# Batch-by-batch order, part of K and V kept on chip, four-byte transposes and column-tiled matmuls in a two-pass attention decode

## The chip, the cores and the metric

The kernel runs on one core of one Trainium2 chip. The metric is the device time of one execution in microseconds (us). A run with "rounds" alternates the kernel under test with the kernel before on the same chip. Ratios are the mean time of one kernel's runs over that of the other's runs of the same rounds, so they are not quite the ratio of the medians quoted.

TensorE does the matrix multiplies; the traces show each as two records, the load of a *stationary* operand and the matmul of a *moving* operand with it (25052 of each in the kernel before). VectorE and ScalarE do elementwise work and in these kernels copy results out of PSUM, TensorE's output memory (640 copies of 691 ns and 384 of 1012 ns for the transposes of the kernel before). GpSimd does the reduction over partitions (256 of them there, 371 or 430 ns each). DMA brings data from HBM, the chip's main memory (557 MB there).

## The reference, cut to what matters

Two identical rounds of attention and a feed-forward network (FFN) on 8 sequences, one token each. The K and V caches are the same in both attention passes, and 268 MB a pass; all else is small.

```python
B, Hq, Hkv, Sk, Dh, D, F = 8, 32, 8, 8192, 128, 512, 1792      # bf16
def attn(x):
    q = (x @ wq).reshape(B, 1, Hq, Dh).transpose(0, 2, 1, 3)
    k = repeat(k_cache, 4, axis=1);  v = repeat(v_cache, 4, axis=1)
    p = softmax(q @ k.T * Dh ** -0.5)
    return (p @ v) ... @ wo
x = x + attn(layernorm(x));  x = x + silu(layernorm(x) @ w1) @ w2
x = x + attn(layernorm(x));  x = x + silu(layernorm(x) @ w1) @ w2
```

One (batch, group) *pair* is a K of 8192 x 128 and a V of the same size, 2.1 MB each, and serves 4 query heads. There are 64 pairs a pass.

## The kernel before: the parts that matter

All 64 pairs of one pass, then the FFN, then all 64 pairs again. K has its positions on partitions when it lands; the scores take it the other way round, so each of its 64 chunks of 128 x 128 goes through TensorE as a bf16 transpose, 8 of them to one tile in PSUM, and is copied out by VectorE or ScalarE. Then K is the *stationary* operand of the scores, and V that of the PV product, with 4 moving columns each.

```python
def emit_tgroup(j, grp):                       # 8 transposes, one copy
    for k in range(CPG):
        pe.transpose(tpv[:, k, :], KNs[kn][:, c, :], ident[:, :])
    # copy of 128x1024 bf16 out of PSUM: ScalarE for groups 1, 4, 7, else VectorE
def emit_scores_group(j, grp):
    pe.matmul(scp[:, c, :], KTs[kt][:, c, :], QT[:, b, g*REP:(g+1)*REP])
...
for t in range(NPAIR + L_PV + 1):
    jp = t - L_PV
    for grp in range(GROUPS):
        emit_tgroup(t + 1, grp)                # K of the next pair
        emit_scores_group(t, grp)              # scores of this pair
        emit_pv_group(jp, grp)                 # PV of two pairs ago
        # softmax steps of pair t-1 at grp 1 and 4 ...
```

What TensorE is given in one step comes from three different pairs. A copy has a whole pair's time to finish before its scores come up.

## Time and profile before

| | before |
|---|---|
| time, median | 1409.9 us (3 runs; 1409.3 after a fourth) |
| bytes read | 557 MB |
| DMA rate over the span; in mid-pass | 400; 417 to 421 GB/s |
| TensorE busy | 90% |
| mean granted TensorE clock | 0.617 |

From the page of the kernel before: busy time of TensorE, then, in 40 slices of the span, the granted clock and DMA's busy share in tenths, the rate moved, the chain of waits by engine, and the two costliest groups of its transposes (busy us, mean ns of one | idle before).

```profile
span 1403.6 us, 53785 instructions
...
PE 1266.5 (90%) x25052; PEld 1235.7 (88%) x25052; DVE 673.8 (48%) x1436; ACT 450.6 (32%) x527; POOL 103.1 (7%) x263
...
PEclk8655556555657667567767855555575555667677
DMA  9999999999999999999499999999999999999981
GB/s 390 395 399 409 420 419 424 425 425 411 421 420 419 418 420 406 425 419 416 161 419 377 427 426 416 416 413 413 409 421 419 420 420 418 423 423 425 422 367 64
...
PE 61%; DMA 36%; issue 2%; DVE 0%; ACT 0%; SPq 0%; ACTq 0%; DVEq 0%
...
L386 PE MATMUL TPp<-ident,arena 128*128 128x128 bf16 x8192 | 937.6, 286 | 29.7 <-DMA arena<-in_A_k_cache_dram 19.0
...
L393 DVE COPY arena<-TPp 128x1024 bf16<-128x1024 bf16 x640 | 440.5, 691 | 505.1 <-PE TPp L386 498.8
```

The table of stretches of the same kernel (stretch and its length; busy us of TensorE, weight loads, VectorE, ScalarE, GpSimd with counts; granted clock, DMA share, GB/s):

```profile
200.00:400.00 200.00, 191.57 (x3760) 190.88 (x3758) 101.35 (x215) 66.67 (x78) 15.57 (x39) 0.57 1.01 421
...
800.00:1000.00 200.00, 200.00 (x3749) 200.00 (x3747) 101.61 (x215) 66.61 (x77) 15.63 (x39) 0.50 1.00 417
```

TensorE and DMA are at their limit at once: DMA moves 417 to 421 GB/s at a share of 1.00, and TensorE is busy without a gap, at half its clock in the second stretch. The chain of waits there, start and length of each piece in us, repeats every 1.28 us:

```profile
300.04 0.87 PE TPp L386 x8
300.91 0.19 PE SCp L439 x8
301.10 0.23 PE OTp L495 x8
301.33 0.87 PE TPp L386 x8
```

Eight such steps make a pair: 10.24 us. Where the clock was granted in full (1.00 from 785 to 788 us, 0.50 from 300 to 310 us), the same group of 8 transposes took half as long (timeline of the kernel before; start, length):

```profile
786.36 0.61 PE L386 MATMUL TPp<-ident,arena 128*128 128x128 bf16 x8 [1.94 <-issue]
786.81 0.34 PE L439 MATMUL SCp<-QT,arena 128*128 128x4 bf16 x8
```

The next group starts 0.45 us after the transposes: 56 ns each.

### The profile page before, as it was taken

The page shows a single profiled execution, that of the slowest core. Times are in us where ns is not written, and L with a number is a line of the kernel's source. Part 1 is how long each engine was busy: PE and PEld are TensorE (multiplying, and loading weights), DVE is VectorE, ACT ScalarE, POOL GpSimd, SP SyncE. Part 2 cuts the span into 40 slices and gives each one's busy share as a digit, 9 for nine tenths or more (in the row PEclk, how much of TensorE's full clock was granted, in tenths as well). Part 3 has the DMA queues.
Part 4 walks back from the last instruction along what each step waited for, and adds up shares of the span by engine and source line. Part 5 has one row for each costly group of instructions (what it writes and reads, how often), then busy time and mean ns, then how long its engine had stood idle before and what let it go on. Part 6 is the DMA issues. An engine that isn't in the chain of part 4 may idle for free.

```text
span 1403.6 us, 53785 instructions
## 1 busy us (share of the span) xinstructions
PE 1266.5 (90%) x25052; PEld 1235.7 (88%) x25052; DVE 673.8 (48%) x1436; ACT 450.6 (32%) x527; POOL 103.1 (7%) x263
## 2 busy tenths in 40 slices
PE   3999999999987888998758899999999999888987
PEld 2999999999987888988538799999999999888984
DVE  1554544554544445555325455555555544445552
ACT  1433323333323323333124333333333333233331
POOL 0000000000000000000000000000000000000000
PEclk8655556555657667567767855555575555667677
DMA  9999999999999999999499999999999999999981
GB/s 390 395 399 409 420 419 424 425 425 411 421 420 419 418 420 406 425 419 416 161 419 377 427 426 416 416 413 413 409 421 419 420 420 418 423 423 425 422 367 64
DMA packets 48767, 560.78 MB, mean 400 GB/s; under 512 B 4240, under 2 KB 14240, under 8 KB 14752
## 3 DMA queue, kind: packets, MB, share of 16 engines
q1 hardware_dynamic: 37440, 541.10, 92.1%
q10 hardware_dynamic: 11104, 16.25, 3.2%
q8 instruction: 196, 3.21, 0.9%
q14 instruction: 27, 0.22, 0.0%
HBM read 557.33 MB, written 0.01 MB: 397 GB/s over the span
## 4 chain that ended last, share of the span: by engine, by line
PE 61%; DMA 36%; issue 2%; DVE 0%; ACT 0%; SPq 0%; ACTq 0%; DVEq 0%
PE TPp L386 38%; DMA arena<-in_A_v_cache_dram 31%; PE OTp L495 12%; PE SCp L439 9%; DMA arena<-in_A_k_cache_dram 5%; PE MISC L544 1%; PE MISC L580 1%; DMA wreg<-in_A_wq_dram 1%; PE MISC L562 0%; DVE X L341 0%; ACT L311 0%; SPq L255 0%; ACT arena L391 0%; DVE xn L317 0%; DVE st_11 L307 0%
## 5 line engine op out<-in xcount | busy, mean ns | idle before, releaser
L386 PE MATMUL TPp<-ident,arena 128*128 128x128 bf16 x8192 | 937.6, 286 | 29.7 <-DMA arena<-in_A_k_cache_dram 19.0
L386 PEld LDWEIGHTS TPp<-ident,arena 128*128 128x128 bf16 x8192 | 712.3, 129 | 30.6 <-DMA arena<-in_A_k_cache_dram 19.2
L393 DVE COPY arena<-TPp 128x1024 bf16<-128x1024 bf16 x640 | 440.5, 691 | 505.1 <-PE TPp L386 498.8
L391 ACT COPY arena<-TPp 128x1024 bf16<-128x1024 bf16 x384 | 388.6, 1012 | 860.5 <-PE TPp L386 860.5
L495 PE MATMUL OTp<-P,arena 128*128 128x4 bf16 x8192 | 366.4, 168 | 70.6 <-DMA arena<-in_A_v_cache_dram 61.7
L439 PEld LDWEIGHTS SCp<-QT,arena 128*128 128x128 bf16 x8192 | 398.4, 111 | 8.9 <-issue 7.4
L439 PE MATMUL SCp<-QT,arena 128*128 128x4 bf16 x8192 | 394.9, 170 | 6.1 <-issue 5.2
L495 PEld LDWEIGHTS OTp<-P,arena 128*128 128x128 bf16 x8192 | 295.8, 102 | 77.6 <-DMA arena<-in_A_v_cache_dram 66.0
L455 POOL PARTITION_ALL_REDUCE mxa<-mxp x128 | 47.4, 371 | 832.9 <-DVE mxp L450 832.9
L460 DVE TENSOR_TENSOR SCs<-SCs,mxa 128x256 f32<-128x256 f32 x128 | 54.5, 426 | 72.5 <-POOL mxa L455 72.5
L481 POOL PARTITION_ALL_REDUCE ssa<-ssm x128 | 55.0, 430 | 430.4 <-DVE ssm L476 430.4
L468 ACT ACTIVATE P<-SCs 128x256 bf16<-128x256 f32 x128 | 53.5, 418 | 31.3 <-DVE SCs L460 31.3
L484 DVE RECIPROCAL rcp<-ssa 128x4 f32<-128x4 f32 x128 | 22.8, 178 | 71.2 <-POOL ssa L481 71.2
L450 DVE TENSOR_REDUCE mxp<-SCs 128x4 f32<-128x256 f32 x128 | 53.8, 420 | 4.3
L447 DVE COPY SCs<-SCp 128x256 f32<-128x256 f32 x128 | 53.1, 415 | 3.2 <-PE SCp L439 3.2
L476 DVE TENSOR_REDUCE ssm<-P 128x4 f32<-128x256 bf16 x128 | 52.4, 409 | 1.6 <-ACT P L468 1.6
L507 DVE TENSOR_TENSOR attnT<-OTp,rcp 128x4 bf16<-128x4 f32 x128 | 21.3, 167 | 10.2 <-PE OTp L495 10.2
L544 PE MATMUL MISC<-wreg,attnT 128*8 128x512 bf16 x64 | 19.1, 472 | 0.5 <-DVE attnT L507 0.5
L326 PEld LDWEIGHTS MISC<-ident,xn 8*128 8x128 bf16 x16 | 0.7, 94 | 20.9 <-DVE xn L317 20.9
L326 PE MATMUL MISC<-ident,xn 8*128 8x8 bf16 x16 | 1.0, 165 | 19.5 <-DVE xn L317 19.5
L544 PEld LDWEIGHTS MISC<-wreg,attnT 128*8 128x8 bf16 x64 | 6.4, 102 | 12.4 <-issue 7.1
L341 DVE TENSOR_TENSOR X<-MISC,X 8x512 bf16<-8x512 f32 x4 | 2.7, 678 | 29.0 <-PE MISC L544 19.3
(26 smaller groups left out, 56.5 us busy)
## 6 DMA issues: line engine op xcount, KB each, us to landing
arena<-in_A_k_cache_dram SPq DMA_DIRECT2D x128, 2048.0 KB, 15.8
arena<-in_A_v_cache_dram SPq DMA_DIRECT2D x128, 2048.0 KB, 20.3
wreg<-in_A_wo_dram ACTq DMA_DIRECT2D x2, 4096.0 KB, 160.6
wreg<-in_A_wq_dram SPq DMA_DIRECT2D x2, 2048.0 KB, 7.5
wreg<-in_A_wq_dram ACTq DMA_DIRECT2D x2, 2048.0 KB, 19.6
w_5<-in_B_w_dram ACTq DMA_DIRECT2D x1, 1792.0 KB, 28.7
w_6<-in_B_w_dram ACTq DMA_DIRECT2D x1, 1792.0 KB, 96.1
X<-in_A_x_dram SPq DMA_DIRECT2D x1, 8.0 KB
```

Of the source, the lines that this page charges most:

```text
L386: lambda k=k, c=c: pe.transpose(tpv[:, k, :], KNs[kn][:, c, :], ident[:, :])
L391: op(act, lambda: act.copy(dst, tpv), reads=[r_TPp[tb]], writes=[r_KTg[kt][grp]])
L393: op(dve, lambda: dve.tensor_copy(dst, tpv), reads=[r_TPp[tb]], writes=[r_KTg[kt][grp]])
L439: lambda c=c: pe.matmul(scp[:, c, :], KTs[kt][:, c, :], rhs, start=True, stop=True)
L447: op(dve, lambda: dve.tensor_copy(SCs[sl][:, :, :], scp), reads=[r_SCp[bank]], writes=[r_SCs[sl]])
L450: lambda: dve.tensor_reduce(mxp[sl][:, :], SCs[sl][:, :, :], AX.X, ALU.max),
L455: lambda: pool.partition_all_reduce(mxa[sl][:, :], mxp[sl][:, :], 128, bass.bass_isa.ReduceOp.max),
L460: lambda: dve.tensor_tensor(SCs[sl][:, :, :], SCs[sl][:, :, :], mxa[sl][:, :].unsqueeze(2).to_broadcast([128, REP, NCH]), ALU.subtract,),
L468: lambda: act.activation(Ps[sl][:, :, :], SCs[sl][:, :, :], ACT.Exp, scale=SM_SCALE),
L476: lambda: dve.tensor_reduce(ssm[sl][:, :], Ps[sl][:, :, :], AX.X, ALU.add),
L481: lambda: pool.partition_all_reduce(ssa[sl][:, :], ssm[sl][:, :], 128, bass.bass_isa.ReduceOp.add),
L495: lambda c=c: pe.matmul(otp, VSs[vs][:, c, :], Ps[sl][:, :, c], start=(c == 0), stop=(c == NCH - 1))
```

## The change

Its intent is to lift both limits. DMA: go batch by batch, so that the second pass of a batch follows soon after its first, and keep 16 quarter-pairs (*units* of 0.524 MB, out of 23 in SBUF) of each batch on chip between the passes. TensorE: transpose K as four-byte words, two bf16 at a time, so that half the transposes are needed; make Q and P the stationary operands and stream K and V, 512 columns at a time, in *column tiles*, that is, matmuls that write rows 32 apart and are meant to work side by side.

The pieces of the new kernel that matter, cut:

```diff
+KEEP = 16                      # units per batch kept for the second pass
+AHEAD = 6                      # pairs of the next batch put before the second pass
+    def do_transposes(n, q):   # one quarter of a pair: one "slot"
+        src = unit(u).bitcast(FP32)
+        for half in range(2):
+            mm([pe.transpose(TP[half][:, 128*m:128*m+128], src[:, (4*half+m)*128:...], ident) for m in range(4)], ...)
+            r_half = res(f"{r_dst.name}_h{half}")
+            if half == 0:
+                op(dve, dve.tensor_copy(o, i), reads=[r_TP[half]], writes=[r_half, r_dst])
+            else:
+                op(act, act.copy(o, i), reads=[r_TP[half]], writes=[r_half, r_dst])
+    def do_scores(n, q):       # 4 matmuls of 512 columns, two column tiles
+        pe.matmul(SC[bk][32*j:32*j+8, :], Q[:, b, g, e, :], kv[:, i*512:(i+1)*512, e])
+    def do_pv(n, v):           # 4 matmuls of 512 columns, four column tiles
+        pe.matmul(PV[32*x:32*x+16, :], PT[:, 4*t+x, ...], vv[:, :, x, :])
...
+    for slot in range(4 * NP + V_LAG + 1):
+        if 0 < slot <= 4 * NP:
+            do_scores(pn, pq)              # the quarter transposed in the slot before
+            if pq == 1: do_max(pn, 0)
+            if pq == 3: do_max(pn, 1); do_exp(pn)
+        side()                             # a step of projection, FFN, next queries
+        do_transposes(n, q)
+        side()
+        if q == 2: do_pt(n - 1)            # P transposed, row sums
+        do_pv(*pv)                         # V of six slots ago
+        side()
+        do_combine(...)
```

The softmax works on 512-column rows in place of 256; the layernorm's 1/sqrt moves from ScalarE to two GpSimd instructions; the weights are loaded once. Loads are cut in four, so that each row of a load is 4 KB in place of 16 KB. The projection, FFN and next queries of a batch (the *middle steps*) are run between slots, for eight batches, and the last FFN at the end.

## The prediction

> **What bounds the kernel now.** Two things, nearly equal. The page counts 560.8 MB moved at a mean of 400 GB/s; in the table of stretches, 200 to 600 us and 800 to 1200 us show the DMA engines fully busy (share 1.00 to 1.01) at 417 to 421 GB/s. In 800 to 1000 us TensorE is also busy 200 of 200 us, at a granted clock of 0.50. The chain of waits there is a cycle of 8 transposes 0.87 us, 8 score matmuls 0.19 us, 8 PV matmuls 0.22 us: 1.28 us, so 10.24 us a (batch, group) pair, against 4.19 MB / 420 GB/s = 9.98 us of DMA. Freeing only one of the two would give little. About 20 us are lost between layers (the slice at 161 GB/s) and some 30 us at the end.
>
> **What the change does to DMA.** K and V of two passes are 536.9 MB. Sixteen units of 0.524 MB are kept per batch, eight batches: -67.1 MB. wq and wo are loaded once: -8.4 MB. Left: 481.8 MB, -14%. But each row of a load shrinks from 16 KB to 4 KB. From the two queues (65 ns for 1.46 KB packets, 552 ns for 14.5 KB) I estimate 10 ns a packet plus 26.6 GB/s an engine: 400 GB/s at 4 KB. [...] At 406 GB/s: 1187 us.
>
> **What it does to TensorE.** Per quarter of a pair ("slot"), 16 bf16 transposes of 109 ns (1.74 us) become 8 four-byte ones; kept K needs none in its second pass (448 of 512 slots transpose). [...] Scores: 4 matmuls of 512 columns, in two column tiles, 0.85 us at half clock if two run at once. PV: four column tiles, 0.43 us. Evacuations are 512 words (estimate 0.6 us each on VectorE and ScalarE, from 415 ns for 256 f32 and 1012 ns for 1024 bf16), waited for in part, 0.3 us. Scores' column tiling, small fp32 matmuls and middle steps: 0.3 us. That is 2.7 us at half clock and about 1.8 us at full, against a DMA mean of 2.3 us a slot. [...] I expect the clock to rise to about 0.75, and DMA to bind by a small margin.
>
> **Critical path.** DMA 1187 us; start 3 us; stalls where 16 of 23 units are held and only 7 stream, 10 us; tail after the last byte (PV, projections, FFN) 20 us. The layer boundary disappears, since the middle steps run between slots. The softmax, now fewer and wider instructions, stays off the path.
>
> Predicted: **1220 us**, 8 in 10 between 1175 and 1310. Faster by over 2%: 0.92; within 2%: 0.04; slower: 0.04.
>
> **What would show it.** Right: about 482 MB; DMA share above 0.95 through the middle at 400 to 410 GB/s; no dip at mid-span; chain mostly DMA into the arena; [...] PE busy well under 90%. Wrong: chain mostly TensorE, waits for the ktring copies before the scores, DMA share below 0.9.
>
> **What would make it wrong.** [...] column tiles that don't overlap; the clock staying at 0.5: each makes TensorE the limit, 1300 to 1450 us. Packets of 4 KB costing less than estimated: 1170 us.

The slot's sum of 2.7 us at half clock was 0.86 + 0.85 + 0.43 + 0.3 + 0.3, and its first term took 8 four-byte transposes to cost what 8 bf16 ones do (8 x 109 ns). The 0.85 and 0.43 us are estimates as well; at the pace of those bf16 transposes, 109 ns for 128 columns, 512 columns are 0.44 us. Measured where the changed kernel's clock was 0.50 (270 to 275 us), the four score matmuls take 1.02 us and the four of PV 0.60 us from first start to last end. The total of 1220 us is 1187 + 3 + 10 + 20 us, the last three as guesses. The 406 GB/s behind the 1187 us was a little above the estimate of 400; the changed kernel's trace has 407 to 409 GB/s from 85 to 100 us, at a DMA share of 1.03.

## The result

The changed kernel is slower: 1956.5 us (4 runs, 1938.5 to 1967.5) against 1409.3 us, ratio 1.386 with a 95% interval of 1.378 to 1.394. The result is correct.

| | before | after |
|---|---|---|
| time, median | 1409.3 us | 1956.5 us |
| bytes read | 557 MB | 482 MB |
| DMA rate over the span | 400 GB/s | 250 GB/s |
| TensorE busy | 90% | 71% |
| granted clock | 0.617 | 0.904 |

The page of the changed kernel, the same lines:

```profile
span 1936.7 us, 30341 instructions
...
PE 1373.5 (71%) x11410; PEld 822.5 (42%) x11410; DVE 701.5 (36%) x1789; ACT 542.7 (28%) x1150; POOL 64.9 (3%) x174
...
PEclk9998879988999888997899978899799988997997
DMA  9975697756977569765796658966598756855970
GB/s 380 374 268 167 214 352 258 235 163 218 383 251 235 179 234 371 235 220 180 261 390 220 214 162 313 339 224 205 167 337 326 241 164 209 301 176 185 361 277 1
...
L574 PE MATMUL TP<-ident,arena 128*128 128x128 f32 x3584 | 551.3, 303 | 0.0
...
L583 DVE COPY ktring<-TP 128x512 int32<-128x512 int32 x384 | 263.7, 687 | 345.2 <-PE TP L574 345.0
```

A stretch of its table, in the same columns as before:

```profile
400.00:700.00 300.00, 214.37 (x1797) 129.11 (x1795) 108.20 (x275) 82.79 (x173) 10.47 (x27) 0.89 0.69 237
```

The bytes fell and the clock rose, as hoped, but nothing is at its limit any more: DMA's share is 0.69 and TensorE is idle more than a quarter of the time. DMA itself is held up: in the view of its queue's own waits (`--waits --engine SP`: us in total, times, longest) the longest is for transposes to free a unit of SBUF.

```profile
SPq L70 <- PE TP L574: 1137.2, 405, 8.2
```

Some order of work must be the limit. (The page's chain of waits covers only some per cent of the span here, so it has to be read off the timeline.) In the timeline the score matmuls of five successive slots start at 1003.58, 1006.26, 1010.14, 1012.82 and 1017.24 us, which is 2.68, 3.88, 2.68 and 4.42 us a slot and 13.66 us a pair. Here is a slot of 2.68 us (start, length, engine and line, out<-in; in brackets the idle time before it, and what ended that):

```profile
1003.58 0.62 PE L599 MATMUL SC<-ktring,Q 128*8 128x512 bf16 x4 [2.46 <-ACT ktring L585]
1004.12 0.85 PEld L574 LDWEIGHTS TP<-ident,arena 128*128 128x128 f32 x8 [0.45 <-issue]
...
1004.82 0.69 DVE L583 COPY ktring<-TP 128x512 int32<-128x512 int32 x1 [2.65 <-PE TP L574]
...
1005.14 0.39 PE L677 MATMUL PV<-arena,PT 128*16 128x512 bf16 x4
...
1005.62 0.58 ACT L585 COPY ktring<-TP 128x512 int32<-128x512 int32 x1 [2.09 <-PE PV L677]
...
1006.26 0.62 PE L599 MATMUL SC<-ktring,Q 128*8 128x512 bf16 x4 [0.72 <-ACT ktring L585]
```

TensorE issues the transposes in 0.85 us (the 0.45 us of "issue" before them are no idle time of TensorE: the score matmuls run from 1003.58 to 1004.20) and PV after them, and has then nothing to do until the scores at 1006.26. VectorE copies the first half for 0.69 us; ScalarE, which stood idle for 2.09 us, starts the second half only when VectorE is done (1004.82 + 0.69 = 1005.51); the scores wait for it. The trace blames PV for ScalarE's wait, since PV's end was the last event before it. The code has another reason: both copies are booked as writers of one tile, `r_dst`, so the second waits for the first, although they write different halves.

And here is the slot of 4.42 us, at the end of a pair:

```profile
999.81 0.69 DVE L612 TENSOR_REDUCE m<-SC 128x1 f32<-128x512 f32 x1 [1.41 <-PE SC L599]
...
1000.99 0.37 POOL L627 PARTITION_ALL_REDUCE mall<-mh  x1 [13.29 <-DVE mh L620]
...
1001.40 0.16 DVE L634 SCALAR_TENSOR_TENSOR junk<-mall,nsel 128x4 f32<-128x4 f32 x1 [0.50 <-POOL mall L627]
...
1001.49 0.69 DVE L583 COPY ktring<-TP 128x512 int32<-128x512 int32 x1
1001.60 0.69 ACT L643 ACTIVATE P<-SC,nb 128x512 bf16<-128x512 f32 x1 [2.50 <-DVE junk L634]
...
1002.28 0.68 ACT L643 ACTIVATE P<-SC,nb 128x512 bf16<-128x512 f32 x1
...
1002.94 0.58 ACT L585 COPY ktring<-TP 128x512 int32<-128x512 int32 x1
```

VectorE got the maximum and its follow-up first, waits for GpSimd, and only at 1001.49 copies the quarter that has been ready since about 1000.4 (700 ns after its transposes began at 999.70). ScalarE does both exponentials before its copy. TensorE idles 2.46 us before the next scores.

The view of waits sums this up (who waited for what: us in total, times, longest):

```profile
PE SC L599 <- ACT ktring L585: 325.8, 241, 3.3
...
PE MISC L395 <- DVE xn L385: 96.1, 18, 10.6
```

With 60.6 us for the same wait on kept tiles, TensorE stood 386 us before scores. The last line is the layernorm of the middle steps. One case of it, from the timeline:

```profile
653.97 0.25 POOL L377 TENSOR_SCALAR ve<-mv 8x1 f32<-8x1 f32 x1 [8.70 <-issue]
...
655.00 0.40 DVE L385 TENSOR_SCALAR xn<-X,mv,rstd 8x512 bf16<-8x512 bf16 x1 [8.13 <-POOL rstd L379]
...
655.46 0.29 PE L395 MATMUL MISC<-identb,xn 8*128 8x8 bf16 x4 [4.92 <-DVE xn L385]
```

VectorE had the statistics ready at 646.27 (the timeline has their last instruction start at 646.10, for 0.17 us); GpSimd started on them at 653.97, with 8.70 us of "issue", that is, of waiting for no other engine. What GpSimd was given before that instruction is seen in the view of its source line (`--source L377`: count; shortest, median and longest ns; first and last start):

```profile
L377 POOLq MODIFY_POOL_CONFIG  x34: 82/85/85, 173.4 to 1906.3; - x34
```

Two of these, by their name changes of GpSimd's configuration, stand before 17 of the 18 layernorms; here they are at 645.22 and 645.25 us, just after a partition reduction. Pairs with middle steps take 25 us, two of them in each batch, against 13.66; part of that is the clock, which is 0.66 to 0.80 in these pairs.

### The profile page after: what moved, and what is told of

The parts are those of the page before. It is cut to its first block, busy times and chain, and to the rows that moved or that the text cites. A ratio compares the mean times of both kernels' runs of the same rounds, so it can differ in the third digit from the quotient of the medians.

```text
span 1936.7 us, 30341 instructions
## 1 busy us (share of the span) xinstructions
PE 1373.5 (71%) x11410; PEld 822.5 (42%) x11410; DVE 701.5 (36%) x1789; ACT 542.7 (28%) x1150; POOL 64.9 (3%) x174
## 5 line engine op out<-in xcount | busy, mean ns | idle before, releaser
L574 PE MATMUL TP<-ident,arena 128*128 128x128 f32 x3584 | 551.3, 303 | 0.0
L574 PEld LDWEIGHTS TP<-ident,arena 128*128 128x128 f32 x3584 | 436.2, 154 | 221.7 <-issue 221.7
L599 PE MATMUL SC<-ktring,Q 128*8 128x512 bf16 x1536 | 258.1, 418 | 328.2 <-ACT ktring L585 325.8
L585 ACT COPY ktring<-TP 128x512 int32<-128x512 int32 x384 | 224.4, 584 | 796.1 <-PE PV L677 368.7
L583 DVE COPY ktring<-TP 128x512 int32<-128x512 int32 x384 | 263.7, 687 | 345.2 <-PE TP L574 345.0
L612 DVE TENSOR_REDUCE m<-SC 128x1 f32<-128x512 f32 x256 | 176.8, 690 | 327.2 <-PE SC L599 327.1
L643 ACT ACTIVATE P<-SC,nb 128x512 bf16<-128x512 f32 x256 | 173.5, 682 | 362.4 <-DVE junk L634 276.9
L677 PE MATMUL PV<-arena,PT 128*16 128x512 bf16 x2048 | 231.1, 410 | 10.7 <-PE PV L677 0.3
L693 PEld LDWEIGHTS MISC<-selc,E 128*128 128x128 f32 x1024 | 127.5, 196 | 32.8 <-DVE rz L664 27.5
L693 PE MATMUL MISC<-selc,E 128*128 128x4 f32 x1024 | 138.6, 259 | 3.3 <-DVE hsT L512 2.5
L599 PE MATMUL SC<-arena,Q 128*8 128x512 bf16 x512 | 91.8, 448 | 60.6 <-ACT arena L585 60.6
L660 PE MATMUL MISC<-ss,sameh 128*128 128x1 f32 x512 | 75.6, 251 | 8.2 <-DVE CH L417 8.2
```

Of the source, the lines that this page charges most:

```text
L574: [lambda m=m: pe.transpose(TP[half][:, 128 * m:128 * m + 128], src[:, (4 * half + m) * 128:(4 * half + m + 1) * 128], ident[:, :]) for m ...
L583: op(dve, lambda: dve.tensor_copy(o, i), reads=[r_TP[half]], writes=[r_half, r_dst])
L585: op(act, lambda: act.copy(o, i), reads=[r_TP[half]], writes=[r_half, r_dst])
L599: lambda e=e, i=i, j=j, bk=bk: pe.matmul(SC[bk][32 * j:32 * j + 2 * REP, :], Q[:, b, g, e, :], kv[:, i * 512:(i + 1) * 512, e], start=(e = ...
L612: op(dve, lambda: dve.tensor_reduce(mm2[:, t:t + 1], SC[bk][:, :], AX.X, ALU.max), reads=[r_SC[bk]], writes=[res(f"m2_{n % 2}_{t}")])
L643: lambda t=t, bk=bk: act.activation(P[:, t, :], SC[bk][:, :], ACT.Exp, bias=nb[:, :], scale=SM_SCALE, accum_out=ss[:, t:t + 1]),
```

## The experiments

The diffs below are shortened, and partly put in words.

Theory A: the limit is a chain through four engines in the order in which they are given their work: transposes, VectorE's copy, ScalarE's copy, scores, with the softmax and the middle steps standing in front of the copies. Rival B: TensorE's own work, above all the four-byte transposes. Rival C: DMA, which the rows of 4 KB or the few free units slow to 250 GB/s.

### The copies made independent

```diff
-  op(dve, copy, reads=[r_TP[0]], writes=[r_half, r_dst]); op(act, copy, reads=[r_TP[1]], writes=[r_half, r_dst])
+  both acquire [r_half, r_dst] before either releases r_dst; r_dst is released once, after both
```

> One edit: ScalarE's copy of the second half of a transposed K quarter no longer waits for VectorE's copy of the first half (they write different halves of the tile). Theory A (the chain transposes, VectorE copy, ScalarE copy, scores, in program order, sets the slot): in the two plain slots of a pair the ScalarE copy starts about 0.3 us earlier, slots of 2.68 us become about 2.35, a pair 13.66 becomes about 13.0, total about 1870 us against 1950. Rival B (TensorE's work itself, slow four-byte transposes): no change. Rival C (DMA, 4 KB rows and 7 free units): no change.

Measured: 1956.1 us, ratio to before 1.386: no change at all, where theory A had expected 1870 us. The mechanism is there, though. In this kernel's timeline ScalarE's copy begins while VectorE's copy still runs, and now its wait is put down to the transposes:

```profile
1009.45 0.68 DVE L585 COPY ktring<-TP 128x512 int32<-128x512 int32 x1
...
1009.86 0.59 ACT L585 COPY ktring<-TP 128x512 int32<-128x512 int32 x1 [1.14 <-PE TP L575]
```

One of the two slots of 2.68 us became 2.32 us (medians over the run). The other became 3.59, and there the transposes themselves ran slower: a group took 1.97 us in place of 1.09, which is what it takes in the changed kernel where the clock was 0.50 (at 273.62 us). Plain pairs now take 12.9 us where the clock is full or nearly so, 0.7 less than before, and 14.2 us where a slot is at half clock. The mean granted clock fell from 0.886-0.904 (the four runs of the changed kernel) to 0.845-0.852. So the time saved was given back to the clock. Why the clock drops in this kernel and not in the other, these runs don't show. By itself this run doesn't decide between A and the rivals.

### Transposes before scores

```diff
   for slot in ...:
+      do_transposes(n, q)
       do_scores(pn, pq) ...
-      do_transposes(n, q)
```

> One edit: within a slot, TensorE gets the transposes of this quarter before the scores of the quarter before, so that a copy has a whole group of transposes more to finish in, and stands before the softmax in VectorE's and ScalarE's queues. Work and bytes are the same. Theory A: slots of 2.68 to 4.42 us become about 2.4, a plain pair about 10 us in place of 13.66, total about 1480 us (the middle steps stay). Rival B: 1950 us, within 2%. Rival C: 1950 us, within 2%.

Measured: 1792.3 us, ratio to before 1.273, so 8% less than the changed kernel, with the same instructions and bytes. Rivals B and C expected nothing, so the order is a limit whatever else is. A plain slot, from the timeline:

```profile
507.18 0.86 PEld L574 LDWEIGHTS TP<-ident,arena 128*128 128x128 f32 x8 [0.44 <-issue]
...
507.87 0.69 DVE L583 COPY ktring<-TP 128x512 int32<-128x512 int32 x1 [1.10 <-PE TP L574]
...
508.20 0.40 PE L599 MATMUL SC<-ktring,Q 128*8 128x512 bf16 x2
...
508.67 0.59 ACT L585 COPY ktring<-TP 128x512 int32<-128x512 int32 x1 [1.20 <-DVE ktring L583]
...
508.97 0.86 PEld L574 LDWEIGHTS TP<-ident,arena 128*128 128x128 f32 x8 [0.44 <-issue]
```

From transposes to transposes it is 1.79 us, where it was 2.68; both copies now end while TensorE is at other work. The expected total of 1480 us was missed by far, since not all slots became plain: the one after a pair's last scores takes 3.29 us (medians over the run), as the softmax still stands before that slot's copies, the one with P's transposes and the combining matmuls 4.0, and the middle steps cost more than before (two pairs of 28 to 31 us a batch).

### 1/sqrt on VectorE in place of GpSimd

```diff
-  pool.tensor_scalar(ve, var, LN_EPS, op0=add);  pool.tensor_tensor(rstd, ve, mhalf, ALU.pow)
+  nine small dve instructions: integer first guess, two Newton steps
```

> One edit: the layernorm's 1/sqrt is made on VectorE (an integer guess and two Newton steps) in place of two GpSimd instructions, which started 7 to 9 us after their input was there. Theory A': the 96 us that TensorE waits for xn (18 times) fall to below 20 us, and the total falls by about 80 us to about 1870. Rival: the middle steps cost by their own matmuls; then less than 20 us.

Measured: 1891.6 us, ratio 1.340: 65 us less than the changed kernel, where about 80 were expected. TensorE's wait for xn falls from 96 to 29 us, of which 18 us are a single wait. The edit also takes out the changes of configuration: the whole trace has 70 MODIFY_POOL_CONFIG records in the changed kernel and 4 here. In the changed kernel's 16 cases of "issue", 133 us in all, GpSimd starts 7.1 to 9.3 us after the change of configuration (8.7 us in the case above, 7.7 us after its input was there). The two instructions themselves take 0.25 and 0.59 us. The run took out the changes and the instructions together, so it shows what both cost, and not the changes alone.

### Nothing kept on chip

```diff
-KEEP = 16
+KEEP = 0
```

> One constant: KEEP 0, so nothing stays on chip between the passes; bytes rise by 67 MB to 549 MB, and all 512 slots transpose. Theory A: bytes are not the limit; only the four pairs per batch at the kept stage lose their shorter slots (mean 10.9 us against 13.66), about 11 us a batch, total about 2040 us, DMA rate up to about 270 GB/s. Rival C (DMA is slow because of small rows, at 250 GB/s): 549 MB at that rate, about 2200 us.

Measured: 2040.4 us, ratio 1.447, as theory A had it. DMA moved 551 MB at 270 GB/s, more than in the changed kernel, so rows of 4 KB were not what held it to 250 GB/s. This run also has more free units; but the order run moved 270 GB/s with the free units as they were, and the fastest version below moves 371, so rival C falls on both counts. Plain pairs take 13.67 us here, as in the changed kernel; what is gone are its shorter pairs, 7.1 to 12.3 us, at the stage where kept K needs no transposes and no copies. So in the changed kernel keeping 67 MB saved that work, and not time on DMA.

### The three edits together, and the exponentials one slot later

```diff
-  if pq == 3: do_max(pn, 1); do_exp(pn)
+  if pq == 3: do_max(pn, 1)
...
+  if q == 1: do_exp(n - 1)        # after do_transposes of that slot
```

> The three edits together: transposes before scores, the two copies of a quarter independent, 1/sqrt on VectorE. Theory A: from the 1792 us of the order edit, the middle steps give back about 65 us as they did alone, the independent copies perhaps 20: about 1700 us. If the edits only moved the same wait about, it stays near 1790.

> The three edits, and the softmax's exponentials of a pair are given to ScalarE (and their bias to VectorE) one slot later, behind the copies of the next transposed quarter. Theory A: the slot after a pair's last scores (3.3 us with the order edit) comes down to about 2 us, a plain pair from 10.9 to about 9.5 us, which is below the 10.3 us that its 4.19 MB take at 406 GB/s, so DMA begins to bind in plain pairs; total about 1500 us. Rival D (after the copies, TensorE's own work is the limit at about 11 us a pair): stays near 1700.

Measured: 1687.9 us (1.201) for the three edits, about the 1700 expected, and 1545.8 us (1.098) with the late exponentials. For these theory A had 1500 us with DMA at its limit in plain pairs, and rival D about 1700; neither came, and DMA moved 314 GB/s in the mean. The slot after a pair's last scores falls from 3.28 us (with the three edits) to 1.80 us. Plain pairs now take 9.4 us (clock 1.00) or 10.9 us (0.84). The mean clock is 0.863.

### bf16 operands for the combining matmuls

```diff
-  E  = PV * rz  in f32;   4 matmuls of f32 operands
+  Eb = PV * rz  in bf16;  4 matmuls of bf16 operands
```

> As before, and the matmuls that combine a pair's output take bf16 operands (4 matmuls, in place of 4 f32 ones that the trace shows as 8, 1.05 us). Theory A: if DMA already binds in plain pairs, no change there, and about 20 us from the middle and kept pairs; if TensorE binds, 0.8 us a pair, 100 us.

Measured: 1380.5 us, ratio 0.981 with an interval of 0.976 to 0.987, and correct: the first version below the kernel before, though by a yardstick of 2% that is still unclear. TensorE's line on the page, before this edit and with it:

```profile
PE 1371.1 (89%) x11410; PEld 833.1 (54%) x11410; DVE 718.2 (47%) x1951; ACT 540.4 (35%) x1150; POOL 49.6 (3%) x138
...
PE 1166.4 (85%) x10898; PEld 674.2 (49%) x10898; DVE 719.4 (52%) x1952; ACT 540.8 (39%) x1150; POOL 49.6 (4%) x138
```

The gain of 165 us is far above what theory A gave it, and above the 100 us of its rival. So TensorE's own work was the limit in this version, not yet DMA: rival B, which the order run refutes as the whole limit of the changed kernel, is right here, once the order is mended. The combining matmuls (4 of f32, which the trace shows as 8 records) fall from 1.05 us to 0.25 us a pair, 102 us in all. The rest, about 60 us, goes with the clock, which rises from 0.863 to 0.931: most plain pairs now take 8.6 us, and it is 0.9 or more in 30 of the page's 40 slices. This edit alters the arithmetic a little, so it is a better kernel and not a test of the given one.

### Middle steps two a slot, and one a slot

```diff
-  side() three times a slot
+  side() twice a slot;   in the second run once a slot, without the empty steps between
```

> As before, and the middle steps (projection, FFN, next queries) are given out two a slot instead of three. Theory A: fewer of their waits fall on TensorE, 2 to 4 us a batch and step group: 30 us less in all. Rival: their cost is TensorE work; no change. Best guess of the four edits and this one: 1350 to 1400 us, DMA busy over 0.85.

> On the fastest version so far (1305 us): the middle steps one a slot, with nothing between them, 16 steps in 17 slots. In the 40 us per batch where they run, DMA moved 320 GB/s against 408 elsewhere; that is about 8.6 us a batch, 70 us in all. Theory A (TensorE waits for their chain of small steps): half of that comes back, about 1270 us. Rival (their TensorE work is what costs): no change, 1300 us.

Measured: 1305.0 us (ratio 0.929, 0.924 to 0.933) for two a slot, the fastest of all; 1315.8 us (0.932) for one a slot. The first edit gained 75 us, where 30 were expected: the steps of a batch, from the projection to the last query step, stretch over 14 slots in place of 9, TensorE's wait for xn falls from 70.5 us (18 times) to 22.5 us (2 times), and the clock rises from 0.931 to 0.953. The second gained nothing, so its expectation failed. It was a weak test, though: with the empty steps gone the steps stretch over 15 slots, hardly more than 14, and the wait for xn stays at 22.3 us. What the rest of the middle steps costs stays open. Compare the page of the version with two a slot,

```profile
PE 1134.6 (87%) x10898; PEld 661.9 (51%) x10898; DVE 717.4 (55%) x1952; ACT 538.6 (41%) x1150; POOL 50.2 (4%) x138
...
PEclk9989899998999998999999988999889989899896
DMA  9999999999999999999999989999999999989991
GB/s 370 385 401 409 324 356 408 408 407 326 380 408 409 396 312 410 408 408 365 363 409 408 409 304 359 408 408 403 316 386 408 408 373 326 376 316 330 404 408 46
```

and two stretches of it, the first with middle steps, the second plain:

```profile
470.00:480.00 10.00, 7.87 (x84) 4.62 (x80) 7.25 (x25) 4.46 (x10) 0.45 (x1) 1.00 0.93 324
520.00:530.00 10.00, 9.77 (x93) 5.93 (x93) 5.87 (x14) 5.68 (x14) 0.37 (x1) 1.00 1.03 409
```

In plain stretches TensorE is busy 9.8 of 10 us at full clock, and DMA moves 409 GB/s at a share of 1.03: both limits are met again. In the middle stretches the rate falls to about 320 GB/s.

### On the fastest version: nothing kept, old order, dependent copies

> On the version at 1305 us: KEEP 0, 67 MB more bytes. In the changed kernel as given this cost 84 us, which theory A put down to transposes, not bytes. Now DMA moves 408 GB/s in most stretches, so bytes should cost: 67 MB / 408 GB/s = 164 us, less what the slower middle stretches hide: about 1430 us. If TensorE is the limit instead: 64 more slots of transposes at 1.0 us, about 1370 us.

> On the version at 1305 us: scores before transposes again, the rest kept. Theory A: TensorE waits for the copies of each quarter again, slots of about 2.3 us, a plain pair 10.5 us or more in place of 8.6, [...]: about 1500 us. If the order no longer matters: 1305 us.

> On the version at 1305 us: ScalarE's copy waits for VectorE's copy again. With transposes before scores the copies have a slot to finish in, so theory A expects no change beyond 1% (1295 to 1320 us).

Measured: nothing kept 1387.9 us (ratio 0.984), scores before transposes again 1432.9 us (1.016), dependent copies again 1317.7 us (0.933). Against the kernel before, the first two are unclear by the yardstick of 2%; what counts here is their distance from 1305 us.

Without kept units DMA is full almost everywhere; one stretch of its table:

```profile
400.00:700.00 300.00, 262.46 (x2536) 156.74 (x2537) 166.59 (x441) 125.73 (x263) 10.59 (x28) 0.98 1.03 408
```

At 408 GB/s its 549 MB take 1345 us, so this version is 43 us above what its bytes need. The expected 1430 us was too high, and the number alone is nearer to the 1370 us expected if TensorE is the limit; but in the stretch shown DMA is full while TensorE is busy 262 of 300 us. With 67 MB less, the kernel doesn't save their 164 us but 83, since it is then held up elsewhere (482 MB at 408 GB/s are 1181 us, and it takes 1305).

The old order costs 128 us even with every other edit in place: slots of 2.32, 3.16, 2.31 and 2.49 us, 10.3 us a pair against 8.6 (medians). That is less than the expected 1500 us, which had counted on a lower clock too; it stayed at 0.965. The dependent copies cost 1%, within what A allowed; the intervals of the two ratios (0.928 to 0.938, and 0.924 to 0.933 for the fastest version) overlap.

## Why the prediction was wrong

It said 1220 us, faster with a chance of 0.92. It was 1956 us. Point by point:

- **The kernel before at two limits: right.** The fastest version ends at the same two limits.
- **Bytes: right.** 482 MB were read, as predicted.
- **DMA at 400 to 410 GB/s with rows of 4 KB: right as a rate, but not the limit of the changed kernel.** Once something else didn't hold it up, DMA ran at 408 to 409 GB/s.
- **"The clock to rise to about 0.75": right in direction.** It rose to 0.904. What sets the clock, these runs don't show. In the kernel before it was 0.50 in one stretch and 1.00 in another, and the fastest version, where four-byte transposes are 504 of TensorE's 1135 busy us, ran at 0.953.
- **Four-byte transposes at 0.86 us for eight at half clock: wrong by nearly a factor of two.** Eight take 0.85 us at full clock (106 ns each, at 1004.12 us) and 1.57 us at half clock (196 ns each; changed kernel at 273.62 us, clock 0.50). At full clock 16 bf16 transposes of 56 ns would take 0.90 us: in TensorE time the four-byte form saves next to nothing. What sets their time, no run separates, nor what this error cost in the changed kernel.
- **"About 1.8 us at full" clock for a slot of TensorE: right for a plain slot, by luck, and too low for the mean.** A plain slot takes 1.79 us once nothing waits. But its transposes take twice the estimate, halved for full clock (0.85 us against 0.43), and it has neither the 0.3 us of waits nor the 0.3 us of small matmuls and middle steps; the errors cancel. The slot with P's transposes, row sums and combining matmuls takes 3.18 us even with bf16 operands. In all TensorE is counted busy 1373.5 us in the changed kernel, 2.68 us for each of 512 slots at a clock of 0.904: already more than the 1220 us predicted for the whole.
- **The risk of "column tiles that don't overlap": did not come.** Four PV matmuls of 410 ns each in the mean are done in 0.39 us (at 1005.14).
- **"Evacuations ... waited for in part, 0.3 us": this is the step that failed.** The sizes of the copies were right: 0.69 and 0.58 us against an estimate of 0.6. What failed was taking them as mostly hidden. The prediction never wrote down the order in which each engine gets its work. In that order the scores of a quarter come right after its copies, the two copies are in series, and at the end of a pair both stand behind the softmax. TensorE idles 0.72 us before the scores in a plain slot and 2.46 us at the end of a pair: 386 us in all, against the 0.3 x 448 = 134 us of the estimate. That is 252 of the 736 us that the prediction missed by. What the chain cost with the softmax and the middle steps in it is seen from the edits of order and waiting, which took 411 us off.
- **"Scores' column tiling, small fp32 matmuls and middle steps: 0.3 us" a slot: too low.** The small f32 matmuls of row sums and combining alone are counted busy 75.6 + 138.6 us, 0.42 us a slot. The middle steps cost two pairs of 25 us and some more in each batch. Two GpSimd instructions, with the changes of configuration before them, are worth 65 us; giving out the steps less densely, 75 us in the version that could use it.
- **"The softmax ... stays off the path": wrong.** It stood in front of the copies in VectorE's and ScalarE's queues. Moving only the exponentials took 142 us off (1687.9 to 1545.8 us).
- **The signs named for a wrong prediction held:** "waits for the ktring copies before the scores, DMA share below 0.9". It was 0.72 on the page.

The prediction thus took a sum of busy times for a slot, 1.8 to 2.7 us, where a chain of waits set it, 3.65 us in the mean (first score matmul to first score matmul, over the run). Of the 3.65 us about 2.7 are busy, so both failed: the overlap, and the sum itself. The same instructions in another order took 164 us less at once; the edits of order and waiting together (order, copies, 1/sqrt, exponentials) took 1956 to 1546 us; with the cheaper combining matmuls and thinner middle steps it is 1305 us, 7% below the kernel before. So the schedule was the larger fault, but not the only one: with the schedule mended and the arithmetic as given, the best version, 1545.8 us, is still 10% slower than the kernel before; it took cheaper combining matmuls as well.

What stays open: why half-clock stretches come in some versions and not in others with like gaps, and so how much of each edit's gain is the clock's.

## What to carry to other kernels

Before adding up an engine's work, write down for each engine the order in which it gets its instructions, and walk one round of the loop: an engine that takes its work in the order given, as TensorE did here, and is fed a producer's result in its very next step, waits for the whole trip through the other engines (386 us before scores in the changed kernel; the other order took 164 us off). Put a stage of other work between a producer and its consumer, as the kernel before did, and put the copies that free the busiest engine ahead of longer work in the queues of the engines that do them. When no engine and no DMA queue is near its limit, look for such a chain, or for one resource name that covers two independent writes, before changing any operation. Once the chain is gone, add up the busiest engine's work again: here it was the next limit.
